# Attention and mixture of experts on one core: loads of q, k and v in pieces by head pair, and another order of TensorE's step

## The chip, the cores and the metric

The kernel runs on one core of a Trainium2 chip. The metric is the device time of one execution in microseconds, taken as the median of the runs.

## The reference

A windowed attention feeds a top-1 mixture of experts. Inputs q, k, v are float32 (8, 8, 576, 64); each token sees itself and the 63 before it.

```python
scores = q @ k.T / sqrt(64);  scores[not (0 <= i - j < 64)] = -1e9
attn = softmax(scores);       x = (attn @ v) as (4608, 512)
logits = (x/|x|) @ (emb/|emb|).T / tau          # 8 experts
e = argmax(logits);           gate = softmax(logits)[e]
out[token] = gate * (relu(x @ w1[e]) @ w2[e])   # w1[e] 512x1024, w2[e] 1024x512
```

## The kernel before

The work has two parts, one after the other. The first goes over the 4608 tokens in 36 tiles of 128 (two blocks of 64 queries each). It is written out by hand as steps: step `s` of `stages(s)` issues, for five tiles at once, the scores of tile `s`, the transposes of its exponentials for tile `s-1`, the values of tile `s-2`, the transposes of x for tile `s-3` and the logits of tile `s-4`. The order in which the calls stand is the order in each engine's queue, and each engine takes its queue strictly in turn. Every stage has one buffer in PSUM only (`score`, `pair`, `back`, `xback`), so a stage of the next step waits until the last step's has been read. Beside that, groups of four tiles get their expert (`choose`), their rank among its tokens (`ranks`, `ranks_out`), and are scattered to DRAM by GpSimd (`place`). The second part, from about 190 us on, runs the experts' two layers over slots of tokens, with weights loaded by SyncE, split into two halves by ScalarE and VectorE, and dense matmuls on TensorE.

What a step gives each engine, with line numbers of the profile of before:

- TensorE: scores (L188), values (L238, L243), logits (L297), transposes of x (L280), transposes of the exponentials (L220), and for some steps ranks (L334, L335).
- ScalarE: `own_scores` copies half of the scores out (L197), `xT_evac` evacuates x transposed (L284), `squares` (L273), `exponentials` (L211).
- VectorE: `all_scores` puts the other half in by a `copy_predicated` (L200), `maxima` (L204), `x_out` divides and writes x (L263 to L265), `attn_halves` masks the transposed exponentials into `aM` (L225), and the small operations on logits and ranks (`logits_out` L306, `choose`, `ranks_out`).
- GpSimd: `less_max` subtracts the maxima (L208), and `place`.

The loads of the first part stand on SyncE's queue. `load_qk(b)` brings q and k of one batch (nine blocks, four and a half steps) in two transfers, `load_v(b)` v in one; there are three buffers for q and k and two for v, and a transfer waits until TensorE has read what stood there. SyncE does nothing else, so nothing but these waits, and one for the landing of the eighth transfer before, holds it in a step.

```python
        for b in range(2, B):
            if s == (NB * (b - QB) + NB - 1) // 2 + 1:
                load_qk(b)
            if s == (NB * (b - VB) + NB - 1) // 2 + 3:
                load_v(b)
```

Here NB is 9, QB 3 and VB 2. One quarter of the experts' first weights (`w1raw`) is loaded in each of steps 7, 16, 25 and 30.

Ahead of the steps, q and k come in two parts (blocks 0 to 3, then the rest), with the constants `cs`, v, the experts' rows `er` (16 KB), `tb` and `ct`, and the last columns of the constants, which VectorE casts into `upper`. `expert_norms()` squares the experts' rows on ScalarE (L406), `expert_emb()` divides them on VectorE, `expert_emb_T()` transposes them on TensorE (L418) through `back`. `warm(n)` issues n small matmuls that nobody reads.

Of the kernel before, what the change touches and what calls it, by code (L numbers as in the profile page):

```python
# [22 lines left out]
B, H, S, D = 8, 8, 576, 64  # L23
N, DM, DF, E = 4608, 512, 1024, 8
WIN = 64
NB = S // WIN
# [56 lines left out]
def attention_moe(ctx, tc, q, k, v, emb, tau, w1, w2, kc, kt, out):  # L83
    nc = tc.nc
# [13 lines left out]
    def weave(*chains):  # L98

        chains = list(chains)  # L100
        while chains:
            chains = [c for c in chains if next(c, chains) is not chains]
# [21 lines left out]
    back, misc = (psa.tile([P, 512], F32, name=nm) for nm in ("back", "misc"))  # L124
# [30 lines left out]
    QB = 3  # L155
    qT, kT = ([aq.tile([P, 4, S], F32, name=f"{nm}{i}") for i in range(QB)] for nm in ("qT", "kT"))
    VB = 2
    vb = [av.tile([P, 4, NB, D + 1], F32, name=f"v{i}") for i in range(VB)]

    def load_qk(b, lo=0, hi=NB, engines=(nc.sync, nc.sync)):  # L160

        for engine, t, src in zip(engines, (qT, kT), (q, k)):
            engine.dma_start(t[b % QB][:, :, lo * WIN:hi * WIN], src[b, :, :, lo * WIN:hi * WIN].rearrange("u p s -> p u s"))

    def load_v(b, lo=0, hi=NB):
        nc.sync.dma_start(vb[b % VB][:, :, lo:hi], v[b, :, :, lo:hi].rearrange("u p a d -> p u a d"))

    def vblock(g):
        return vb[g // NB % VB][:, :, g % NB]
# [25 lines left out]
    def own_scores(T):  # L195
        sm[T] = ap.tile([P, 4, 2, WIN], F32, name="sm", bufs=3)
        nc.scalar.copy(sm[T], sv[:, :, :, 1])  # L197
# [4 lines left out]
    def maxima(T):  # L202
        st[T] = ap.tile([P, 8], F32, name="st", bufs=2)
        nc.vector.reduce_max(out=st[T], in_=sm[T].rearrange("p u h c -> p (u h) c"), axis=AX.X)  # L204

    def less_max(T):
        t = sm[T].rearrange("p u h c -> p (u h) c")
        nc.gpsimd.tensor_tensor(out=t, in0=t, in1=st.pop(T).unsqueeze(2).to_broadcast([P, 8, WIN]), op=ALU.subtract)  # L208
# [13 lines left out]
    def attn_halves(T):  # L222

        aM[T] = ap.tile([P, 2, 4, P], F32, name="aM", bufs=2)
        nc.vector.tensor_tensor(out=aM[T], in0=pT.pop(T).unsqueeze(1).to_broadcast([P, 2, 4, P]),  # L225
                                in1=halves.unsqueeze(2).to_broadcast([P, 2, 4, P]), op=ALU.mult)
# [3 lines left out]
    def values(T):  # L230

        px[T] = pair
        m = aM.pop(T)
        o, p = m[:, 0], m[:, 1]
        for u in range(4):
            for hp, z in sides:
                g, pr, pz = 2 * T + z, slice(64 * hp, 64 * hp + 64), slice(64 * z, 64 * z + 64)
                nc.tensor.matmul(pair[pz, hp, u * (D + 1):(u + 1) * (D + 1)], lhsT=o[pr, u, pz],  # L238
                                 rhs=vblock(g)[pr, u], start=True, stop=g % NB == 0)
            for hp, z in sides:  # L240
                g, pr, pz = 2 * T + z, slice(64 * hp, 64 * hp + 64), slice(64 * z, 64 * z + 64)
                if g % NB:
                    nc.tensor.matmul(pair[pz, hp, u * (D + 1):(u + 1) * (D + 1)], lhsT=p[pr, u, pz],  # L243
                                     rhs=vblock(g - 1)[pr, u], start=False, stop=True)
# [37 lines left out]
    def xT_evac(T):  # L282
        xT[T] = ap.tile([P, 4, P], F32, name="xT", bufs=2)
        nc.scalar.copy(xT[T], pxT.pop(T))  # L284
# [15 lines left out]
    def in_rows(G):  # L300

        return x_rows(*GROUPS[G])[:, :, C_LOG:C_LOG + E]

    def logits_out(G):
        a, b = GROUPS[G]
        nc.vector.tensor_copy(in_rows(G), plv[:, G % 2, :b - a])  # L306
# [51 lines left out]
    def rank_rows(G):  # L358
        a, b = GROUPS[G]
        n = b - a  # L360
        rk = ap.tile([P, n, E], F32, name="rk")
        at = [cs[:, K_E:K_E + E], *late][sum(a >= cut for cut in CUTS)]
        nc.vector.tensor_tensor(out=rk, in0=rank.pop(G), in1=at.unsqueeze(1).to_broadcast([P, n, E]), op=ALU.add)
        yield
        nc.vector.tensor_tensor(out=rk, in0=rk, in1=ohs.pop(G), op=ALU.mult)
        yield
        pos = ap.tile([P, n], F32, name="pos")
        nc.vector.reduce_sum(out=pos, in_=rk, axis=AX.X)
        yield
        rks[G] = ap.tile([P, n], I32, name="pi")  # L370
        nc.vector.tensor_copy(rks[G], pos)
        yield

    def ranks_out(G):
        weave(rank_rows(G))
# [14 lines left out]
    def root_guess(ss, t1):  # L390
        nc.gpsimd.tensor_tensor(out=t1, in0=ss, in1=half[:ss.shape[0]], op=ALU.pow)

    def root_refine(ss, t0, t1, o):

        nc.vector.tensor_scalar(out=t0, in0=t1, scalar1=1e-30, scalar2=None, op0=ALU.max)
        nc.vector.reciprocal(t1, t0)
        nc.vector.scalar_tensor_tensor(out=t1, in0=ss, scalar=t1, in1=t0, op0=ALU.mult, op1=ALU.add)
        nc.vector.tensor_scalar(out=o, in0=t1, scalar1=0.5, scalar2=1e-6, op0=ALU.mult, op1=ALU.add)
# [6 lines left out]
    def expert_norms():  # L405
        nc.scalar.activation(esq, er, AF.Square, accum_out=es[:, 0:1])  # L406
        root_guess(es[:, 0:1], es[:, 2:3])

    def expert_emb():
        root_refine(es[:, 0:1], es[:, 1:2], es[:, 2:3], es[:, 3:4])  # L410
        nc.vector.tensor_tensor(out=es[:, 0:1], in0=es[:, 3:4], in1=tb, op=ALU.mult)
        nc.vector.reciprocal(es[:, 1:2], es[:, 0:1])
        nc.vector.tensor_scalar(out=er2, in0=er, scalar1=es[:, 1:2], scalar2=None, op0=ALU.mult)
# [17 lines left out]
    def warm(n, to=back):  # L431

        for _ in range(n):
            nc.tensor.matmul(to[:, :P], lhsT=ones, rhs=ones, start=True, stop=True)

    def stages(s):

        def there(d):
            return 0 <= s - d < NT

        def ending(d):
            return [G for G, (a, b) in enumerate(GROUPS) if b + d == s]

        scores(s)
        if s < 3:
            warm(20, misc)
        own_scores(s)
        if there(2):
            tokens(s - 2)
            values(s - 2)  # L450
        if there(4):
            logits(s - 4)
        if there(3):
            x_transposes(s - 3)
            xT_evac(s - 3)
        all_scores(s)
        maxima(s)
        less_max(s)
        if there(3):
            squares(s - 3)  # L460
        for G in ending(3):
            logits_out(G)
        if there(2):
            x_out(s - 2)
        if s < 3:
            warm(20, misc)
        if there(1):
            attn_transposes(s - 1)
            attn_halves(s - 1)
        for G in ending(4):  # L470
            ranks(G)
            ranks_out(G)
        for G, (a, b) in enumerate(GROUPS):
            for T in range(a, b):
                if s == (T + 8 if b - a == 4 else b + 4):
                    place(T)
        for G in ending(3):
            choose(G)
            count(G)
        if s in wsplit:  # L480
            split_hi(wsplit[s], w1raw, w1h)
        exponentials(s)
        if s in wsplit:
            split_lo(wsplit[s], w1raw, w1h, w1l, nc.vector)
        if 1 <= s < 7:
            blanks(s - 1)

        for b in range(2, B):
            if s == (NB * (b - QB) + NB - 1) // 2 + 1:
                load_qk(b)  # L490
            if s == (NB * (b - VB) + NB - 1) // 2 + 3:
                load_v(b)
        for f in wsteps.get(s, ()):
            f()

# [422 lines left out]

    load_qk(0, 0, 4, (nc.sync, nc.scalar))
    nc.sync.dma_start(cs, kc[:, :K_U])  # L920
    load_v(0, 0, 4)
    load_qk(0, 4, NB, (nc.sync, nc.scalar))
    nc.sync.dma_start(er, emb)
    nc.sync.dma_start(tb, tau.to_broadcast([E, 1]))
    nc.sync.dma_start(ct, kt)
    nc.sync.dma_start(xbuf[2][:, :P], kc[:, K_U:])
    load_v(0, 4, NB)
    load_qk(1)
    load_v(1)
    nc.vector.memset(ones, 1.0)  # L930
    nc.vector.memset(low, -BIG / 64)
    nc.vector.memset(half, 0.5)
# [3 lines left out]
    nc.gpsimd.memset(xall[:, :, C_SS + 1:], 0.0)  # L936
    nc.gpsimd.memset(xmore[:, :, C_SS + 1:], 0.0)
    warm(60)
    expert_norms()

    buffers("xb", 2, [P, DM], F32, const)
    for name, shape, dtype in (("xh", [P, 4, 2 * P], F32R), ("xl", [P, 4, 2 * P], F32R)):
# [2 lines left out]
    for t in range(NT - 1):  # L945
        stages(t)
        if t == 0:
            nc.vector.tensor_copy(upper, xbuf[2][:, :P])
            expert_emb()
        if t == 1:  # L950
            expert_emb_T()
        if t == CUTS[0] + 4:
            sum_counts(CUTS[0])
            begin_late(0, counts("early"))
        if t == 30:
            load_x(0)
            load_x(1)
        if t in (32, 33):
            x_parts(t - 32)
# [4 lines left out]
    T, G = NT - 1, len(GROUPS) - 1  # L964
# [202 lines left out]
```

## Time and profile before

| | |
|---|---|
| time, median of 3 runs | 650.78 us (649.51 to 652.6) |
| profiled execution, own time / span | 653.34 / 651.6 us |
| busy: TensorE, VectorE, ScalarE, GpSimd | 93%, 68%, 51%, 31% of the span |
| mean granted TensorE clock | 0.978 |
| SyncE's queue (q1) | 120.08 MB, 56.8% of 16 engines |
| fetches of instructions (q8) | 58, 0.95 MB, 0.6% |
| one load: q, k, v of a batch | 1152 KB, 1152 KB, 1170 KB |
| one load: a quarter of w1 | 512 KB |

The profile is of one execution. A row of a timeline has the start, the time taken, the engine, the line, the operation, out<-in, and in brackets how long the engine had stood idle and what ended that. "issue" means that it waited for nothing that the profile shows. In a table of waits stand the microseconds in total, their number and the longest. In a table by stretches each engine has its busy time and the number of its instructions, and at the end stand the granted clock, the share of the DMA engines' time, and GB/s. The span is a little shorter than the execution's own time, which has what lies around it.

### The profile page before, as it was taken

The page shows a single profiled execution, that of the slowest core. Times are in us where ns is not written, and L with a number is a line of the kernel's source. Part 1 is how long each engine was busy: PE and PEld are TensorE (multiplying, and loading weights), DVE is VectorE, ACT ScalarE, POOL GpSimd, SP SyncE. Part 2 cuts the span into 40 slices and gives each one's busy share as a digit, 9 for nine tenths or more (in the row PEclk, how much of TensorE's full clock was granted, in tenths as well). Part 3 has the DMA queues.
Part 4 walks back from the last instruction along what each step waited for, and adds up shares of the span by engine and source line. Part 5 has one row for each costly group of instructions (what it writes and reads, how often), then busy time and mean ns, then how long its engine had stood idle before and what let it go on. Part 6 is the DMA issues. An engine that isn't in the chain of part 4 may idle for free. (4 is left out here: it accounts for less than half of the span.)

```text
span 651.6 us, 18205 instructions
## 1 busy us (share of the span) xinstructions
PE 605.4 (93%) x7178; PEld 541.9 (83%) x7178; DVE 443.3 (68%) x884; ACT 334.8 (51%) x513; POOL 202.0 (31%) x242
## 2 busy tenths in 40 slices
PE   6887888788789989999999999999999999999996
PEld 5776777677679978998998998998889988998984
DVE  1676895889968965767646887557665877567623
ACT  1343453445445244747544766547565576547533
POOL 1224544545464422322222331222122231222111
PEclk9998997989979999999999999999999999999999
DMA  9865476554442459987688688684798867694351
GB/s 286 323 226 212 162 274 218 210 210 159 148 152 80 162 129 301 304 283 229 212 255 291 220 268 288 211 293 157 244 301 267 288 194 271 201 305 175 116 163 36
DMA packets 83901, 143.77 MB, mean 221 GB/s; under 512 B 14421, under 2 KB 37717, under 8 KB 83808
## 3 DMA queue, kind: packets, MB, share of 16 engines
q1 hardware_dynamic: 76176, 120.08, 56.8%
q0 software_dynamic: 6000, 19.18, 7.5%
q10 hardware_dynamic: 1632, 3.28, 1.4%
q8 instruction: 58, 0.95, 0.6%
q14 instruction: 35, 0.29, 0.1%
HBM read 123.23 MB, written 20.05 MB: 220 GB/s over the span
## 5 line engine op out<-in xcount | busy, mean ns | idle before, releaser
L774 PE MATMUL ph<-xl,w1h 128*128 128x256 f32 x576 | 162.8, 283 | 2.0 <-POOL xl L676 2.0
L774 PE MATMUL ph<-xh,w1h 128*128 128x256 f32 x576 | 163.4, 284 | 0.0
L774 PE MATMUL ph<-xh,w1l 128*128 128x256 f32 x576 | 162.6, 282 | 0.0
L834 PE MATMUL po<-w2h,hl 128*128 128x512 f32 x312 | 122.9, 394 | 0.0
L834 PE MATMUL po<-w2h,hh 128*128 128x512 f32 x312 | 122.5, 393 | 0.0
L834 PE MATMUL po<-w2l,hh 128*128 128x512 f32 x312 | 122.3, 392 | 0.0
L844 POOL DMA_INDIRECT out<-o,rest x39 | 49.7, 1273 | 221.1 <-ACT o L843 215.7
L788 DVE SCALAR_TENSOR_TENSOR hl<-ph,hh 128x512 fp32r<-128x512 f32 x78 | 53.3, 689 | 93.5 <-ACT hh L784 93.3
L152 DVE TENSOR_TENSOR w2l<-w2raw,w2h 128x1024 fp32r<-128x1024 f32 x80 | 94.8, 1219 | 26.4 <-ACT w2h L149 26.2
L774 PEld LDWEIGHTS ph<-xl,w1h 128*128 128x128 f32 x576 | 109.9, 191 | 3.3 <-POOL xl L676 2.6
L774 PEld LDWEIGHTS ph<-xh,w1h 128*128 128x128 f32 x576 | 109.9, 191 | 1.2 <-issue 0.3
L774 PEld LDWEIGHTS ph<-xh,w1l 128*128 128x128 f32 x576 | 109.8, 191 | 0.0
L149 ACT CAST w2h<-w2raw 128x1024 fp32r<-128x1024 f32 x80 | 81.9, 1050 | 41.6 <-PE po L834 34.4
L152 DVE TENSOR_TENSOR w1l<-w1raw,w1h 128x1024 fp32r<-128x1024 f32 x80 | 95.5, 1248 | 11.2 <-ACT w1h L149 10.9
L676 POOL TENSOR_TENSOR xl<-xt,xh 128x512 fp32r<-128x512 f32 x39 | 51.1, 1312 | 103.1 <-ACT xh L672 103.1
L149 ACT CAST w1h<-w1raw 128x1024 fp32r<-128x1024 f32 x80 | 78.3, 1047 | 1.8 <-DMA w1raw<-in_w 1.8
L784 ACT ACTIVATE hh<-ph 128x512 fp32r<-128x512 f32 x78 | 46.0, 595 | 54.2 <-PE ph L774 39.3
L834 PEld LDWEIGHTS po<-w2h,hl 128*128 128x128 f32 x312 | 58.6, 188 | 13.0
L834 PEld LDWEIGHTS po<-w2l,hh 128*128 128x128 f32 x312 | 58.6, 188 | 12.7
L834 PEld LDWEIGHTS po<-w2h,hh 128*128 128x128 f32 x312 | 58.6, 188 | 12.2
L238 PE MATMUL pair<-v,aM 64*64 64x65 f32 x1152 | 40.2, 231 | 25.7 <-DVE aM L225 19.6
L238 PEld LDWEIGHTS pair<-v,aM 64*64 64x64 f32 x1152 | 33.6, 139 | 33.3 <-DVE aM L225 26.1
(171 smaller groups left out, 835.2 us busy)
## 6 DMA issues: line engine op xcount, KB each, us to landing
w2raw<-in_w SPq DMA_DIRECT2D x80, 512.0 KB, 6.0
w1raw<-in_w SPq DMA_DIRECT2D x76, 512.0 KB, 5.0
xb<-xs SPq DMA_DIRECT2D x156, 64.0 KB, 5.5
v<-in_v SPq DMA_DIRECT2D x7, 1170.0 KB, 5.6
qT<-in_q SPq DMA_DIRECT2D x7, 1152.0 KB, 6.7
kT<-in_k SPq DMA_DIRECT2D x7, 1152.0 KB, 9.3
w1raw<-in_w ACTq DMA_DIRECT2D x4, 512.0 KB, 4.4
v<-in_v SPq DMA_DIRECT2D x1, 650.0 KB, 5.0
```

What stands on the lines that cost most here:

```text
L149: nc.scalar.copy(hi[c], raw[c])
L152: eng.tensor_tensor(out=lo[c], in0=raw[c], in1=hi[c].bitcast(F32), op=ALU.subtract)
L238: nc.tensor.matmul(pair[pz, hp, u * (D + 1):(u + 1) * (D + 1)], lhsT=o[pr, u, pz], rhs=vblock(g)[pr, u], start=True, stop=g % NB == 0)
L676: nc.gpsimd.tensor_tensor(out=xl, in0=t, in1=xh.bitcast(F32), op=ALU.subtract)
L774: nc.tensor.matmul(o, lhsT=ww[c][:, f * P:(f + 1) * P], rhs=xx[:, c, :n], start=(c == 0 and i == 0), stop=(c == 3 and i == 2))
L784: nc.scalar.activation(hh, ph[g, part], AF.Relu)
L788: nc.vector.scalar_tensor_tensor(out=hl, in0=ph.pop((g, part)), scalar=0.0, in1=hh.bitcast(F32), op0=ALU.max, op1=ALU.subtract)
L834: nc.tensor.matmul(po[a], lhsT=xx[:, f, at], rhs=ww[f // 2][:, f % 2], start=(f == 0 and i == 0), stop=(f == 7 and i == 2))
L844: d = nc.gpsimd.indirect_dma_start(out=out, out_offset=bass.IndirectOffsetOnAxis(ap=tok, axis=0), in_=o, in_offset=None, bounds_check=N - ...
```

## The change

Four things are changed, and no arithmetic. The four transfers of head pairs that make up a batch's q, k or v become transfers of their own (`load_u` issues q and k of one pair, `load_vu` v of one pair), and a table `loads` puts them into steps: the four pairs of q and k into four steps in a row, the four of v into two. The small loads (`er`, `tb`, `ct`) go ahead of v and of the second part of q. The experts' norms go from ahead of step 0 to behind it, `expert_emb` and `expert_emb_T` one step later each. And the calls in a step stand in another order.

```diff
+    def load_u(b, u):
+        for t, src in ((qT, q), (kT, k)):
+            nc.sync.dma_start(t[b % QB][:, u], src[b, u])
+    def load_vu(b, u):
+        nc.sync.dma_start(vb[b % VB][:, u], v[b, u])
+    loads = {}
+    for b in range(2, B):
+        s0 = max(1, (NB * (b - QB) + NB - 1) // 2 + 1)
+        for u in range(4):
+            loads.setdefault(s0 + u, []).append(lambda b=b, u=u: load_u(b, u))
+        s0 = (NB * (b - VB) + NB - 1) // 2 + 3
+        for u in range(4):
+            loads.setdefault(s0 + u // 2, []).append(lambda b=b, u=u: load_vu(b, u))
...
             tokens(s - 2)
-            values(s - 2)
         if there(4):
             logits(s - 4)
         if there(3):
             x_transposes(s - 3)
-            xT_evac(s - 3)
+        if there(2):
+            values(s - 2)
+        for G in ending(3):
+            logits_out(G)
         all_scores(s)
         maxima(s)
+        if s < 3:
+            warm(20, misc)
+        if there(3):
+            xT_evac(s - 3)
         less_max(s)
...
         if there(1):
             attn_transposes(s - 1)
-            attn_halves(s - 1)
         for G in ending(4):
             ranks(G)
             ranks_out(G)
+        if there(1):
+            attn_halves(s - 1)
...
+        for f in loads.get(s, ()):
+            f()
...
     nc.sync.dma_start(cs, kc[:, :K_U])
-    load_v(0, 0, 4)
-    load_qk(0, 4, NB, (nc.sync, nc.scalar))
     nc.sync.dma_start(er, emb)
     nc.sync.dma_start(tb, tau.to_broadcast([E, 1]))
     nc.sync.dma_start(ct, kt)
+    load_v(0, 0, 4)
+    load_qk(0, 4, NB, (nc.sync, nc.scalar))
     nc.sync.dma_start(xbuf[2][:, :P], kc[:, K_U:])
     load_v(0, 4, NB)
-    load_qk(1)
-    load_v(1)
+    for u in range(4):
+        load_u(1, u)
+    for u in range(4):
+        load_vu(1, u)
...
     warm(60)
-    expert_norms()
...
         if t == 0:
             nc.vector.tensor_copy(upper, xbuf[2][:, :P])
+            expert_norms()
+        if t == 1:
             expert_emb()
-        if t == 1:
+        if t == 2:
             expert_emb_T()
```

The line numbers of the changed kernel are 17 to 19 higher. ScalarE's queue at the start, before: the square of the experts (into `xr`, where their rows lie) is ahead of the first copy of scores.

```order
L406 ACTIVATE xr,es<-xr 8x512
L197 COPY sm<-score 128x512
L211 ACTIVATE sm<-sm 128x512
L197 COPY sm<-score 128x512
L211 ACTIVATE sm<-sm 128x512
```

And now:

```order
L214 COPY sm<-score 128x512
L228 ACTIVATE sm<-sm 128x512
L423 ACTIVATE xr,es<-xr 8x512
L214 COPY sm<-score 128x512
L228 ACTIVATE sm<-sm 128x512
```

The square has moved behind the first tile's copy and exponential.

SyncE's queue from the q and k of batch 5 to those of batch 6, before (128 partitions, four head pairs, 576 tokens in one transfer):

```order
L163 DMA qT_118<-in_q 128x4x576
L163 DMA kT_121<-in_k 128x4x576
L166 DMA v_122<-in_v 128x4x585
L424 DMA w1raw_101<-in_w 128x1024
L163 DMA qT_116<-in_q 128x4x576
```

And now:

```order
L171 DMA qT_118<-in_q 128x576
L171 DMA kT_121<-in_k 128x576
L171 DMA qT_118<-in_q 128x576
L171 DMA kT_121<-in_k 128x576
L174 DMA v_122<-in_v 128x585 x2
L171 DMA qT_118<-in_q 128x576
L171 DMA kT_121<-in_k 128x576
L441 DMA w1raw_101<-in_w 128x1024
L174 DMA v_122<-in_v 128x585 x2
L171 DMA qT_118<-in_q 128x576
L171 DMA kT_121<-in_k 128x576
L171 DMA qT_116<-in_q 128x576
```

The last two pairs of q and k have moved behind pieces of the next v on the queue; every transfer is a quarter as long.

TensorE's queue in one step, from its scores to its transposes of exponentials, before (L238 and L243 are the values, `misc` holds the logits, `xback` x, `back` the exponentials):

```order
L188 MATMUL score<-kT_120,qT_117 64x128 x16
L238 MATMUL pair<-v_122,aM 64x65 x4
L243 MATMUL pair<-v_122,aM 64x65 x4
...
L297 MATMUL misc<-embT,xT 64x8 x8
L280 MATMUL xback<-cs,xr 128x128 x4
L220 MATMUL back<-cs,sm 128x128 x4
```

And now:

```order
L205 MATMUL score<-kT_120,qT_117 64x128 x16
L314 MATMUL misc<-embT,xT 64x8 x8
L297 MATMUL xback<-cs,xr 128x128 x4
L255 MATMUL pair<-v_122,aM 64x65 x4
L260 MATMUL pair<-v_122,aM 64x65 x4
...
L237 MATMUL back<-cs,sm 128x128 x4
```

The values have moved behind logits and x; scores and exponentials stand where they stood.

More of the change, by code (lines that the diff above doesn't have):

```diff
@@ L460, in stages @@
             squares(s - 3)
-        for G in ending(3):
-            logits_out(G)
         if there(2):
             x_out(s - 2)
-        if s < 3:
-            warm(20, misc)
         if there(1):
             attn_transposes(s - 1)
-            attn_halves(s - 1)
         for G in ending(4):
@@ L486, in stages @@
             blanks(s - 1)
[L488 to L492, printed above, removed]
+        for f in loads.get(s, ()):
+            f()
         for f in wsteps.get(s, ()):
```

## The prediction

> **What bounds the kernel now.** I read the page first, then the sums of waits, then VectorE's instructions step by step, and last the transfers around TensorE's waits. The page, the granted clock (40 slices of 16.3 us):
>
> ```profile
> PEclk9998997989979999999999999999999999999999
> ```
>
> After slice 12 the clock is full and TensorE (93% of the span) is the bound; the change leaves that part alone, so whatever the first 190 us gain or lose comes out at the end one for one. The dips are all in the attention steps. The sums of waits there:
>
> ```profile
> ACT xT L284 <- PE xback L280: 68.8, 31, 6.1
> DVE sm L200 <- ACT sm L197: 25.0, 19, 12.2
> PE pair L238 <- DVE aM L225: 19.6, 27, 1.9
> PE pair L238 <- issue: 6.1, 4, 2.2
> ```
>
> TensorE waits for VectorE in most steps, VectorE only now and then for ScalarE. So VectorE sets the steps' pace, and its own busy time is the floor. Rows of `copy_predicated` (L200, once a step) for steps 4, 13, 17 and 32, and VectorE's busy time (the pair of numbers after PEld) between the first and the last:
>
> ```profile
> 33.19 0.74 DVE L200 COPY_PREDICATED sm<-cs,score 128x512 f32<-128x512 uint32 x1 [0.22 <-ACT sm L197]
> 78.94 0.72 DVE L200 COPY_PREDICATED sm<-cs,score 128x512 f32<-128x512 uint32 x1
> 97.15 0.72 DVE L200 COPY_PREDICATED sm<-cs,score 128x512 f32<-128x512 uint32 x1
> 173.84 0.73 DVE L200 COPY_PREDICATED sm<-cs,score 128x512 f32<-128x512 uint32 x1
> 33.19:173.84 140.65, 116.64 (x3372) 102.75 (x3369) 114.32 (x243) 66.84 (x144) 64.35 (x104) 0.94 0.58 202
> ```
>
> Steps 13 to 17 took 18.21 us, 4.55 each, with no stall in them. 28 steps at 4.55 would be 127.4; they took 140.65. So 13.2 us of steps 4 to 32 are stalls. Where they are: the loads that the DMA queue issues, and TensorE's waits for nothing that the profile shows ("issue"):
>
> ```profile
> 34.89 0.39 SPq L163 DMA_DIRECT2D qT<-in_q  x1
> 44.03 0.39 SPq L166 DMA_DIRECT2D v<-in_v  x1
> 44.47 1.61 SPq L424 DMA_DIRECT2D w1raw<-in_w  x1
> 50.76 0.38 SPq L163 DMA_DIRECT2D qT<-in_q  x1
> 66.35 0.37 SPq L166 DMA_DIRECT2D v<-in_v  x1
> 95.85 0.37 SPq L163 DMA_DIRECT2D qT<-in_q  x1
> 123.04 0.37 SPq L163 DMA_DIRECT2D qT<-in_q  x1
> ...
> 43.15 0.28 PE L238 MATMUL pair<-v,aM 64*64 64x65 f32 x2 [1.23 <-issue]
> 52.80 0.29 PE L238 MATMUL pair<-v,aM 64*64 64x65 f32 x5 [0.60 <-issue]
> 59.28 0.37 PE L238 MATMUL pair<-v,aM 64*64 64x65 f32 x2 [2.08 <-issue]
> 103.56 0.38 PE L238 MATMUL pair<-v,aM 64*64 64x65 f32 x4 [2.17 <-issue]
> 130.39 0.29 PE L297 MATMUL misc<-embT,xT 128*64 128x8 f32 x5 [1.41 <-issue]
> ```
>
> Each wait but one stands 7 to 9 us behind a q load (a k load follows each at once: 2 x 1152 KB, 2.36 MB together); the 0.60 stands behind v with w1raw (1.7 MB). The v load alone (1.2 MB, at 66.35) is followed by none. What TensorE lacks are instructions. The transfers in 53.4 to 56.8 us (first two rows), and in 52 to 57 us (last):
>
> ```profile
> DMA packets 617, 1.38 MB, mean 407 GB/s; under 512 B 16, under 2 KB 16, under 8 KB 617
> q1 hardware_dynamic: 617, 1.38, 103.3%
> ...
> q8 instruction: 1, 0.02, 1.4%
> ```
>
> For 3.4 us nothing but q and k moved, 38 packets on each of 16 engines; only then came the one fetch of instructions (q8), too late for 57.2 us, where TensorE ran dry. The clock pays again (last three numbers: granted clock, DMA share, GB/s):
>
> ```profile
> 57.00:66.00 9.00, 6.92 (x138) 6.31 (x133) 4.01 (x7) 2.31 (x5) 3.56 (x5) 0.62 0.34 125
> 130.00:136.00 6.00, 5.61 (x118) 5.16 (x117) 3.96 (x11) 2.31 (x5) 2.47 (x6) 0.72 0.54 210
> ```
>
> The five waits sum to 7.5 us; the other 5.7 of the 13.2 are half clock and the refilling of the chain.
>
> **Part 1, the loads.** Twelve pieces of 0.29 MB for three transfers of 1.2 MB per batch. Bytes stay. SyncE isn't paced by the steps: it issues q and k of batch b as soon as the scores of b-3 free the buffer, at 0.37 to 0.5 us an issue. So the first two head pairs (four pieces, 1.18 MB over 1.8 us) still leave in one burst, of the size of a v load, which costs nothing now. The next v piece waits for TensorE's values and holds the other two pairs behind it on SyncE; nobody misses them, since they have eight steps until use (batch 4: freed in step 8, read in step 18). Then eight pieces, 2.38 MB, leave over some 3.4 us. In that time 407 GB/s drain about 1.0 MB (I allow 0.9 us until they flow), so the backlog peaks near 1.35 MB, between v alone (no wait) and v with w1raw (0.60). I take 0.4 us of loss for each of six such bursts, 2.4 in all: nearest to v's rows. Ends: 0, and 2.6 each (13.2 over five), if peak size means nothing. Term: -13.2 + 2.4 = -10.8.
>
> [...]
>
> **Part 2, the start.** Rows of TensorE, ScalarE and VectorE (`copy_predicated` of steps 0, 1 and 3), the issue of the constants' last columns and their landing (6.7 us later), and the mean times (ns, behind the busy us) of `attn_halves`, maxima and `x_out`:
>
> ```profile
> 6.31 1.10 PE L188 MATMUL score<-kT,qT 64*64 64x64 f32 x32
> 12.43 0.63 ACT L406 ACTIVATE xr<-xr 8x512 f32<-8x512 f32 x1 [9.09 <-DMA xr<-in_emb]
> 13.65 0.72 DVE L200 COPY_PREDICATED sm<-cs,score 128x512 f32<-128x512 uint32 x1 [12.22 <-ACT sm L197]
> 17.39 0.73 DVE L200 COPY_PREDICATED sm<-cs,score 128x512 f32<-128x512 uint32 x1
> 29.28 0.74 DVE L200 COPY_PREDICATED sm<-cs,score 128x512 f32<-128x512 uint32 x1 [1.36 <-ACT sm L197]
> 6.69 0.44 SPq L926 DMA_DIRECT2D xr<-in_kc  x1
> ...
> L225 DVE TENSOR_TENSOR aM<-back,cs 128x1024 f32<-128x1024 f32 x35 | 42.6, 1216 | 6.5 <-PE back L220 6.2 <-PE misc L335 0.2
> L204 DVE TENSOR_REDUCE st<-sm 128x8 f32<-128x512 f32 x36 | 24.7, 686 | 3.6
> L265 DVE TENSOR_TENSOR xr<-pair,sums 128x512 f32<-128x512 f32 x26 | 18.0, 691 | 1.1 <-DVE sums L264 0.2
> ...
> xr<-in_kc SPq DMA_DIRECT2D x1, 64.0 KB, 6.7
> ```
>
> The first scores are ready at 7.4, but ScalarE's square of the experts (L406) stands ahead of their copy and waits for its DMA until 12.43. Moved behind step 0, it frees copy and `copy_predicated` at about 8.0, 5.6 us earlier. What is late next: VectorE's cast of `upper`, in order ahead of step 1, needs the constants' last columns, which land at 13.4 as now (the same bytes stand ahead of them). The three small loads that now go ahead of v and of q's second part cost SyncE some 1.5 us of issues (0.5 each), but not a packet: the engines have work queued all through (share 1.00 in the row below). GpSimd's root of the experts moves behind its subtraction of step 0, where it idles. So step 1's `copy_predicated` comes at 13.6 instead of 17.39. Step 2's stands behind 0.73 + 0.69 + 1.22 of step 1 and the experts' chain (17.39 - 13.65 less 0.72 and 0.69 leaves 2.3 for `upper` and that chain; I take 2.1 for the chain), with gaps at 18.5. Then `expert_emb_T` on TensorE, now behind step 2's transposes, waits until `attn_halves` has read `back`: VectorE gets there at 22.5 (18.5, plus copy 0.73, maxima 0.69, `x_out` 0.69 and its two small operations, halves 1.22, and gaps), and transposes, scores (1.1) and ScalarE's copy follow: step 3's at some 24.8 against 29.28, 4.5 earlier. Against that, the queues are full:
>
> ```profile
> 5.00:31.00 26.00, 19.55 (x430) 17.45 (x430) 11.51 (x24) 5.61 (x11) 4.63 (x9) 0.93 1.00 346
> ```
>
> TensorE, now ahead, asks for its instructions while every engine is taken (share 1.00), where before it did so later. I take 1.5 off, one wait of the rows above. Term -3.0; ends -5.6 (the whole of the copy's advance) and 0.
>
> **Part 3, the step's order.** Values now come behind logits and x. Before, ScalarE's evacuation of x (L284) waits for TensorE, and square and exponential queue behind it:
>
> ```profile
> 53.80 1.04 POOL L208 TENSOR_TENSOR sm<-sm,st 128x512 f32<-128x512 f32 x1 [0.36 <-DVE sums L263]
> 55.56 0.62 ACT L211 ACTIVATE sm<-sm 128x512 f32<-128x512 f32 x1
> ```
>
> The exponential could have started at 54.84 and did at 55.56. With x transposed while TensorE used to wait for `aM`, it starts when GpSimd is done. That shortens the chain to the next copy by up to 0.7 us, but VectorE's busy time is 114.32 / 28 = 4.08 a step, about 4.3 with the gaps between instructions, against 4.55 now: at most 0.25 x 28 = 7 us. I take a third, since in most steps VectorE already runs without a wait: -2.5. Values end some 1.2 us later; VectorE needs them after `copy_predicated` and maxima, 1.5 us behind `aM`, so they stay hidden; if logits and x did not fit into TensorE's wait, each step would lose what doesn't fit. The filler matmuls (`warm`, steps 0 to 2 alone) keep their count: 0. `logits_out` ahead of `copy_predicated`, `ranks_out` ahead of `attn_halves`: same VectorE work, producers done earlier, 0. Steps 33 to 35 and the expert part: 0, within 1.5 either way for where the clock dips there.
>
> **Sum.** -10.8 - 3.0 - 2.5 = -16.3. The profiled execution took 653.3 us (span 651.6), 2.6 above the median of 650.8, which I take for scatter between runs: 637.0 for itself, 634.5 for the median.
>
> **Rivals.**
> A. All stalls go and the start keeps its lead: -13.2 - 4.5 - 4 = -21.7, 629. For it: v's bursts cost nothing now. Against: the second burst is larger than v's.
> B. The fetch's wait doesn't hang on how much is queued, so splitting changes nothing there, or the pieces rush out as one queue all the same: -3.0 - 2.5, 645. If an engine turned to the other queue after a packet or a few, each fetch would wait about as long in both kernels. Against: 38 packets an engine went by before the fetch. [...]
> C. Slower: the second burst of each batch stalls the fetch in full as q and k do now, and the first one too. Eleven bursts at 2.6 are 28.6 against 13.2, net of the gains +9.9: 660. It decides from (13.2 + 5.5) / 2.6, more than seven full stalls, on. For it: 2.38 MB in a row; against: they come over 3.4 us, not one.
> D. B, and the start's lead lost to full queues: 648 to 651, no change.
>
> **Numbers.** The forecast 0.60, A 0.15, B 0.14, C 0.05, D 0.06. Half a per cent (3.3 us) is about what a measurement of this kernel can tell from none. Faster 0.89, same 0.06, slower 0.05. The range goes from within A (626) to B (646) and leaves out C, D and the edge of A.
>
> **What would show it.** Step 0's copy on ScalarE at about 7.5 and VectorE waiting for the constants' DMA at `upper`; TensorE's waits on "issue" in the attention steps 3 us or less instead of 7.5, the clock at 1.00 from 35 to 170 us; `copy_predicated` of step 32 near 158; the wait of `xT` for TensorE far below 68.8. Wrong it is if "issue" waits of 2 us stand behind the v bursts (C), or behind the first pieces (B), or if VectorE begins to wait for `pair` in every step.

## The result

| | before | after |
|---|---|---|
| time, median | 651.3 us (649.51 to 652.6, 4 runs) | 634.88 us (632.41 to 636.99, 4 runs) |
| in a second comparison | 651.79 us (11 runs) | 639.23 us (633.79 to 642.02, 6 runs) |
| profiled execution, own time / span | 653.34 / 651.6 us | 635.14 / 633.4 us |

The ratio is 0.9748 [0.9705, 0.9791], and 0.9783 [0.974, 0.9827] in the second comparison: 14 to 16 us faster by the ratios. The forecast was 634.5; the first median stands 0.4 from it, the second 4.7. The profile after, granted clock in 40 slices, then the sums of waits that answer to those of before:

```profile
PEclk9997999999899999999999999999999999999999
ACT xT L301 <- PE xback L297: 13.8, 23, 2.5
DVE sm L217 <- ACT sm L214: 13.0, 10, 7.5
```

ScalarE's wait for x fell from 68.8 to 13.8 us, and the dips are fewer, not gone. The rows of `copy_predicated` (now L217) of steps 0, 1, 3, 4, 13, 17 and 32, with the cast of `upper` ahead of step 1:

```profile
8.92 0.73 DVE L217 COPY_PREDICATED sm<-cs,score 128x512 f32<-128x512 uint32 x1 [7.49 <-ACT sm L214]
13.91 0.23 DVE L965 CAST upper<-xr 128x128 bf16<-128x128 f32 x1 [3.54 <-DMA xr<-in_kc]
14.05 0.72 DVE L217 COPY_PREDICATED sm<-cs,score 128x512 f32<-128x512 uint32 x1
23.94 0.74 DVE L217 COPY_PREDICATED sm<-cs,score 128x512 f32<-128x512 uint32 x1 [1.55 <-ACT sm L214]
27.83 0.75 DVE L217 COPY_PREDICATED sm<-cs,score 128x512 f32<-128x512 uint32 x1 [0.20 <-ACT sm L214]
68.90 0.73 DVE L217 COPY_PREDICATED sm<-cs,score 128x512 f32<-128x512 uint32 x1
86.50 0.73 DVE L217 COPY_PREDICATED sm<-cs,score 128x512 f32<-128x512 uint32 x1
158.36 0.72 DVE L217 COPY_PREDICATED sm<-cs,score 128x512 f32<-128x512 uint32 x1
```

Step 4 comes at 27.83 against 33.19 (-5.4). Steps 4 to 32 take 130.53 us against 140.65 (-10.1). From step 32 to the end it is 475.0 against 477.8 (-2.7). Together -18.2 between these two executions. Steps 13 to 17 take 17.60, 4.40 each against 4.55. So 28 steps without a stall would be 123.2, and 7.3 us of stalls are left of 13.2.

TensorE's waits on "issue" between 25 and 155 us did not go: 3.0, 2.5 and 1.2 against 6.1, 1.4 and 0.6.

```profile
PE pair L260 <- issue: 3.0, 2, 1.9
PE misc L314 <- issue: 2.5, 2, 1.7
PE score L205 <- issue: 1.2, 2, 0.9
PE pair L255 <- DVE aM L242: 1.6, 4, 0.5
```

Those for `aM` did: 1.6 us, against 12.8 of before between the same times.

The longest wait on issue, and SyncE's queue ahead of it:

```profile
36.00 0.81 SPq L174 DMA_DIRECT2D v<-in_v  x2
38.51 0.43 SPq L441 DMA_DIRECT2D w1raw<-in_w  x1
40.84 0.43 SPq L171 DMA_DIRECT2D kT<-in_k  x1
41.62 0.33 SPq L171 DMA_DIRECT2D qT<-in_q  x1
43.86 0.33 SPq L171 DMA_DIRECT2D kT<-in_k  x1
...
45.89 0.28 PE L260 MATMUL pair<-v,aM 64*64 64x65 f32 x3 [1.86 <-issue]
```

Five rows stand for the thirteen transfers issued from 36.00 on. The second burst (four pieces of batch 2's v, four of batch 3's q and k, w1raw) ends at 41.3, and batch 4's first four pieces, whose buffer has just come free, follow at 41.62: 4 MB in 8 us. The transfers from 40.0 to 43.4 us, and the fetch among those from 43.4 to 45.0:

```profile
q1 hardware_dynamic: 497, 1.25, 100.3%
...
q8 instruction: 1, 0.02, 3.8%
```

For 3.4 us nothing but loads moved, as before the change. The prediction had the two bursts apart.

### The profile page after: what moved, and what is told of

Same layout as the page of the kernel before. It is cut to its first block, busy times and chain, and to the rows that moved or that the text cites. A ratio compares the mean times of both kernels' runs of the same rounds, so it can differ in the third digit from the quotient of the medians.

```text
span 633.4 us, 18301 instructions
## 1 busy us (share of the span) xinstructions
PE 605.2 (96%) x7178; PEld 536.0 (85%) x7178; DVE 441.1 (70%) x884; ACT 336.4 (53%) x513; POOL 202.5 (32%) x242
## 5 line engine op out<-in xcount | busy, mean ns | idle before, releaser
L225 POOL TENSOR_TENSOR sm<-sm,st 128x512 f32<-128x512 f32 x36 | 37.5, 1041 | 67.3 <-DVE sums L280 35.0
L688 ACT CAST xh<-xt 128x512 fp32r<-128x512 f32 x39 | 24.2, 620 | 59.7 <-DVE xt L677 58.9
```

The lines of the kernel that those rows point to most:

```text
L688: nc.scalar.copy(xh, t)
```

## The experiments

The times of before beside them were 652.15 us (the first four), 651.79 (the next four), 653.67 (aligned and shifted) and 653.66 (the last). The sums of waits on issue are TensorE's, between 25 and 155 us.

**The parts, each alone.** Before with the new start:

```diff
     nc.sync.dma_start(cs, kc[:, :K_U])
+    nc.sync.dma_start(er, emb)
+    nc.sync.dma_start(tb, tau.to_broadcast([E, 1]))
+    nc.sync.dma_start(ct, kt)
     load_v(0, 0, 4)
...
-    expert_norms()
...
             nc.vector.tensor_copy(upper, xbuf[2][:, :P])
+            expert_norms()
+        if t == 1:
             expert_emb()
...
```

> Before with the changes at the start alone: small loads ahead of v, the experts' norms behind step 0, expert_emb and expert_emb_T a step later each. My theory: the changed kernel's copy_predicated of step 4 came at 27.83 us against 33.19, so the start is worth 5.4 us, 646 against 651.3; the prediction had 3.0. Rival (the start's lead is given back in the steps behind it, since TensorE asks for its instructions while the DMA engines are full): 649 to 651. Either way the five waits on issue stay about as they were, 7.5 us in sum.

646.0 us, ratio 0.9917 [0.9884, 0.995]: -5.4. Step 4's `copy_predicated` came at 27.54. The lead isn't given back.

Before with the loads in pieces:

```diff
-                load_qk(b)
...
-                load_v(b)
+        for f in loads.get(s, ()):
+            f()
...
```

> Before with the loads of q, k and v in pieces by head pair, spread over steps, and nothing else. My theory (fetches of instructions queue behind what the loads have put into the DMA engines; smaller bursts, shorter waits): 6 us of stalls go, 645; the prediction's term was 10.8, 640.5. Rival (the pieces run together, since the second half of a batch's pieces and the first of the next leave back to back, and the waits of the changed kernel, 6.75 us against 7.5, show that splitting gains nothing): 650 to 652, with four to six waits of 1 to 2 us on issue.

648.7 us, ratio 0.9925 [0.9883, 0.9967]: -4.9, between theory and rival. Steps 4 to 32 took 135.78 us, 8.4 above 28 x 4.55. The waits on issue sum to 5.1 us, against 8.1 in before.

Before with the new order:

```diff
-            values(s - 2)
...
             logits(s - 4)
...
             x_transposes(s - 3)
...
+            values(s - 2)
...
-            attn_halves(s - 1)
...
             ranks(G)
...
+            attn_halves(s - 1)
```

> Before with the new order of the calls in a step and nothing else. My theory: 0.15 us a step over 28 steps (4.55 to 4.40 in the steps without a stall) and some 2 us at the end of the steps: 645 to 647, with copy_predicated of steps 13 and 17 about 17.6 us apart. Rival (the order is what gains the middle, since TensorE then has work that doesn't hang on aM and stalls cost the chain less): 10 us, 641, with the loads and their waits on issue as before.

651.08 us, ratio 1.0005 [0.9973, 1.0036]: nothing, and both expectations missed. Where nothing stalls, a step is shorter: steps 27 to 30 took 13.69 us against 14.31. Steps 13 to 17 took 18.39, not 17.6, with two waits on issue (1.4 and 0.7) in them. The waits sum to 6.7 us, no more than the 8.1 of before; what grew is the time at half clock. The clock and the stretch of steps 4 to 32:

```profile
PEclk8888997979999999999999999999999999999999
33.65:173.31 139.66, 122.88 (x3358) 103.08 (x3355) 114.22 (x244) 70.05 (x147) 65.15 (x104) 0.91 0.58 202
```

139.66 us less 28 x 4.40 leaves 16.5 of stalls, against 13.2 in before. The granted clock is 0.91 there against 0.94.

The new start and the new order, with the large loads of before:

```diff
-        for f in loads.get(s, ()):
-            f()
+        for b in range(2, B):
+            if s == (NB * (b - QB) + NB - 1) // 2 + 1:
+                load_qk(b)
+            if s == (NB * (b - VB) + NB - 1) // 2 + 3:
+                load_v(b)
...
```

> The changed kernel with the large loads of before (one transfer for q, one for k, one for v of a batch, at their old steps). My theory: the stalls of the large loads come back, 6 us, so 641 against 634.9. Rival (splitting gains nothing, the start and the order carry the whole): 634 to 636, the same as the changed kernel, with waits on issue of 7 us in sum.

642.86 us, ratio 0.9883 [0.9849, 0.9916]: -7.6. Theory 1 holds: by the ratios the changed kernel is 6.5 to 8.8 us faster than this one, so the pieces carry that much on top of start and order. Its waits on issue, which sum to 12.6 us; the three largest groups:

```profile
PE pair L243 <- issue: 4.4, 3, 2.0
PE xback L280 <- issue: 3.6, 2, 3.0
PE score L188 <- issue: 2.8, 2, 1.6
```

The changed kernel has 6.7. Steps 4 to 32 took 136.96 us here and 130.53 there, at the same granted clock of 0.96: 6.4 us, about what the waits differ by. Beside the kernel with the new start alone (646.0), this one tells the order's worth with large loads: 2 to 3 us, not clear of noise.

The new start and the pieces, with the old order of a step (the diff of the order alone, the other way round):

> The changed kernel with the old order of the calls in a step (new start, loads in pieces). What is open: start -5.4, loads -4.9 and order +0.3, each alone, sum to -10.0, the whole change gave -16.4. Theory 1 (the parts don't add because the order leaves TensorE no slack: it shortens a step by 0.15 us where nothing is late, and loses that again where fetches are late; with smaller bursts there is less to lose): 641, so that the order is worth 6 here though nothing alone; steps 13 to 17 at 4.55 us each. Rival (start and loads add to more than their sum, since a start 5 us earlier also moves the fetches against the bursts; the order is worth nothing): 635 to 637, with steps of 4.55.

643.82 us, ratio 0.987 [0.9825, 0.9915], against 639.23 of the changed kernel beside it: the order is worth 4.6 here by medians, 5.7 by the ratios. This speaks for theory 1, but the intervals just overlap. The waits on issue sum to 5.8 us; with large loads, the new start and the old order they were 7.6.

**Where the fetches stand.** The changed kernel itself, nothing edited, once more:

> The changed kernel itself, beside the others on the same chip: 635 (ratio 0.975). Its waits on issue need not stand at the same steps as in the first profile if small shifts in time decide them; their sum should be about 6.75 us again.

639.23 us, as above, 4 over what was expected. The execution that was profiled took 642.02, 6.9 above the first, with almost the same waits (7.4 us on issue against 6.7) but more of the slow clock. TensorE's busy time is the number behind the window's length, the granted clock the third from the end. Three stretches of the first execution, then four of this one:

```profile
44.19:47.60 3.41, 1.71 (x59) 1.60 (x63) 2.21 (x6) 1.04 (x3) 1.97 (x6) 0.99 1.04 394
47.60:51.01 3.41, 3.41 (x53) 2.73 (x48) 3.20 (x8) 0.59 (x1) 1.38 (x2) 0.50 0.47 178
51.01:54.43 3.42, 3.42 (x80) 2.97 (x84) 1.52 (x5) 1.84 (x4) 2.23 (x3) 0.51 0.22 80
```

```profile
47.78:51.19 3.41, 2.12 (x55) 1.55 (x51) 2.94 (x6) 1.79 (x4) 1.50 (x3) 1.00 0.79 303
51.19:54.60 3.41, 2.82 (x50) 2.36 (x53) 1.36 (x4) 0.63 (x1) 2.10 (x3) 0.50 0.25 85
54.60:58.02 3.42, 3.42 (x49) 2.74 (x44) 1.98 (x3) 0.59 (x1) 0.00 (x0) 0.50 0.01 4
58.02:61.43 3.41, 3.41 (x77) 2.95 (x80) 1.53 (x5) 1.89 (x4) 2.23 (x3) 0.50 0.46 100
```

In these records the clock changed only at the edges of windows of 3.41 us, all on one grid within an execution: in the first one at 47.56, 54.39, 91.93 and 95.35 us (2, 11 and 1 windows apart), in before at 59.09, 65.92, 103.47 and 110.29 (2, 11 and 2). The grid lies elsewhere in each. Here a window in which TensorE was busy for 1.71 or 2.12 us of 3.41 was followed by windows at half speed, though no single wait reached 2 us. The six executions differ in the same way: the two with a mean clock of 0.994 took 633.8 and 634.5 us, the four with 0.980 to 0.983 took 638.6 to 642.0.

The changed kernel with each fetch moved half a step against the loads:

```diff
-    warm(60)
+    for _ in range(124):
+        nc.tensor.matmul(back[:, :64], lhsT=ones, rhs=ones[:, :64], start=True, stop=True)
```

> The changed kernel with 124 filler matmuls of 64 columns in place of 60 of 128 at the start (the same time, 6.2 us), so that every fetch of TensorE's instructions, one for each 256 of them, comes 128 instructions, about half a step, earlier against the loads. Theory 1 (where a fetch falls in a burst decides how late it is): other waits on issue at other steps, and a time 2 to 5 us away from the changed kernel's, 630 to 640, either way. Rival (the waits are set by the loads alone): the same time within 1 us, 634 to 636.

641.84 us, ratio 0.9805 [0.9752, 0.9858]. The waits moved, now 1.8 us at 49.5 and 2.2 us at 96.9, and sum to 6.4. By the ratios the time is 1.4 above the kernel beside it (0.9783), too little to tell from the scatter. It shows that the place moves, not what it costs.

The changed kernel, with SyncE held to the steps:

```diff
             tokens(s - 2)
+            if s in loads:
+                nc.gpsimd.memset(tick[:, s:s + 1], 0.0)
...
+        if s >= 2 and s in loads:
+            nc.sync.dma_start(ticks[s:s + 1], tick[:, s:s + 1])
         for f in loads.get(s, ()):
```

> The changed kernel, and SyncE made to keep to the steps: ahead of each step's loads from step 2 on stands a transfer of 4 bytes from a word that GpSimd sets in that step, so that SyncE can't issue a step's loads before it. Theory 1 (the second half of a batch's pieces and the first of the next leave together, 3 to 4 MB in a row, and the fetches of instructions wait behind them): waits on issue of 2 us or less in sum where the changed kernel had 6.75, and 3 to 5 us faster than it, 630 to 632 against 635. Rival (the fetches wait for any load, however short the queue): 634 to 636 and some 6 us of waits on issue. It could also be slower, if v then comes late: TensorE's values waiting for the DMA of v.

635.8 us, ratio 0.9753 [0.9715, 0.979]: not to be told from the changed kernel. The waits on issue still sum to 6.2 us (nine, the longest 1.5), so theory 1 missed here. Fetches still waited here, behind the short queue that one step's pieces make; one case is in the transfers from 50.1 to 52.2 us, loads and GpSimd's scatter (q0) with no fetch among them (it began at 52.2), and the wait that followed:

```profile
q1 hardware_dynamic: 269, 0.54, 76.1%
q0 software_dynamic: 36, 0.15, 18.1%
...
54.52 0.27 PE L255 MATMUL pair<-v,aM 64*64 64x65 f32 x2 [0.52 <-issue]
```

How little delay it takes can be estimated from the traces. In all profiles but that of the last kernel below, the waits on issue over 0.15 us between 20 and 190 us, 71 of them, end 1.2 to 1.6 us behind the landing of a fetch of 16 KB, and they stand at multiples of 128 matmuls (each with its weight load: 256 instructions) from each other, within five. (The profile after has 58 such fetches, 0.95 MB, for 7178 matmuls and 7178 weight loads.) The next fetch never began less than 1.0 us behind such a wait, and a fetch took 0.9 us at the least. So, as an estimate which takes the next block's fetch to be asked for when TensorE enters a block of 256 instructions, a fetch that nothing holds up is ready some 3.1 to 3.5 us after that (1.0, 0.9 and 1.2 to 1.6). A block lasts some 4.7 us where nothing stalls (28 steps of 4.38 us in the kernel below hold 3360 matmuls). That leaves 1.2 to 1.6 us: by this estimate a shorter queue still makes TensorE wait as soon as it holds the fetch up for longer.

If it holds, what matters is not only how much is queued but whether the fetch comes before it or behind it. The next kernel schedules the loads for that. `LOADS` gives for each block of 256 instructions the place of a step where TensorE enters it and the pieces to release there; `ungate` stands behind `xT_evac`, `less_max`, `squares` and `exponentials`:

```diff
+    LOADS = {
+        ('lm', 15): (14, [['v', 4, 0], ['v', 4, 1], ['v', 4, 2]]),
...
+    def ungate(spot, s):
+        if (spot, s) in LOADS:
+            i, pieces = LOADS[spot, s]
+            if spot == "lm":
+                nc.gpsimd.memset(tick[:, i:i + 1], 0.0)
+            else:
+                nc.scalar.copy(tick[:, i:i + 1], half[:1])
+            nc.sync.dma_start(ticks[i:i + 1], tick[:, i:i + 1])
+            for p in pieces:
+                load_one(*p)
```

> The changed kernel with a schedule of its loads by TensorE's fetches instead of by steps: q, k, v and w1raw of steps 3 to 30 in pieces (of 0.29 MB, w1raw 0.5), three or four to each block of 256 instructions of TensorE, released by a 4-byte transfer as in the paced kernel, whose word is set by GpSimd or ScalarE at that place of a step which stands within 0.9 us of the moment when TensorE enters a block and asks for the next one. The fetch so starts ahead of the pieces, and they have some 4 us to drain before the next. Theory 1 (a fetch waits for what the loads have queued ahead of it): waits on issue of 1.5 us or less in sum between 25 and 155 us, against 6.2 to 7.4 in the changed and the paced kernel, no half clock there, 28 steps at 4.4 us, and 628 to 632 us. Rival (the wait is the fetch's own latency, or the stalls only move to VectorE and GpSimd): 5 us or more of waits on issue, or 634 to 638 us.

629.68 us (627.59 to 632.07), ratio 0.9647 [0.961, 0.9683], as theory 1 had it, and below both intervals of the changed kernel. It is the fastest version here. Its waits on issue, its steps 4 to 32 with a clock of 1.00, and one release (w1raw and a piece of q, 0.8 MB) with what moved from 101.3 to 103.6 us, the fetch among it:

```profile
PE score L243 <- issue: 0.6, 1, 0.6
```

```profile
28.34:151.00 122.66, 113.18 (x3360) 94.94 (x3359) 113.44 (x243) 71.13 (x163) 65.29 (x113) 1.00 0.78 247
```

```profile
100.96 0.25 SPq L219 DMA_DIRECT2D ticks<-tick  x1
101.26 0.33 SPq L178 DMA_DIRECT2D w1raw<-in_w  x1
101.64 0.44 SPq L182 DMA_DIRECT2D qT<-in_q  x1
...
q8 instruction: 1, 0.02, 2.4%
```

28 steps took 4.38 us each, as the steps without a stall did in the changed kernel (4.40). The paced kernel, also without half clock there, took 128.84: 6.2 us more, with 5.6 us more of waits on issue.

The same pieces, released half a block later:

> The same schedule of pieces as in the aligned kernel, each release about 2.3 us later, half a block of TensorE's instructions, so that the next fetch comes while the pieces drain. Theory 1: the fetches wait again, 5 us or more on issue in sum between 25 and 155 us, 634 to 641 us, slower than the aligned kernel by 4 to 8. Rival (what helps is the even spread, three pieces at a time, and not where they stand against the fetches): the same as the aligned kernel within 2 us.

638.35 us, ratio 0.9782 [0.9746, 0.9817], 8.7 slower than the aligned kernel, with the same pieces in the same groups: the place of the releases alone (and with it which engine sets each word). The waits on issue are 3.5 us against 0.6, less than the 5 that were expected, and one for `kT` grew from 1.0 to 2.1. Steps 4 to 32 took 128.74, 6.1 more. A fetch asked for at about 103.5 us, by the estimate above: the transfers until 106.3, with no fetch among them, and TensorE behind it:

```profile
q1 hardware_dynamic: 257, 0.53, 57.6%
q0 software_dynamic: 80, 0.27, 23.8%
...
108.80 0.29 PE L293 MATMUL pair<-v,aM 64*64 64x65 f32 x5 [1.43 <-issue]
```

GpSimd's scatter (q0, 23.8%) is among them too. Of what else lies between the two, the records show one window at half clock in step 31, at 150.5 us, and two behind step 32, at 171 and 222; the aligned kernel has one behind step 32, at 156, and none from step 4 to there.

The aligned kernel with the old order in a step:

> The aligned kernel with the old order of the calls in a step; its releases are put anew to the moments at which TensorE, in that order, enters a block. What is open: the order alone gave nothing (ratio 1.0005), though a step without a stall took 4.40 us with it and 4.55 without. Theory 1 (the order's 0.15 us a step is real and is lost again only where fetches come late, because TensorE then has no other waits to hide them in): with next to no late fetches the whole 28 x 0.15 = 4.2 us shows, and some 2 us at the end of the steps, so this kernel takes 634 to 636 against 629.7 of the aligned one. Rival (the order is worth nothing at all, and the shorter steps are paid elsewhere): 629 to 631.

641.46 us, ratio 0.9822 [0.9787, 0.9857], 11.8 slower than the aligned one: the rival falls, but the size is twice theory 1's. The profile puts 5.7 us of waits here on issue too, but these are of another kind. All ten ahead of values, 5.5 us of them, end within 0.06 us behind VectorE's `aM`, and nine of them have no fetch that landed 1.2 to 1.6 us before. One of them, with `aM` done at 71.79:

```profile
70.57 1.22 DVE L280 TENSOR_TENSOR aM<-back,cs 128x1024 f32<-128x1024 f32 x1
71.84 0.35 PE L293 MATMUL pair<-v,aM 64*64 64x65 f32 x8 [0.81 <-issue]
```

So fetches are hardly ever late here, and TensorE waits for VectorE, as in before. Steps 4 to 32 and 13 to 17:

```profile
27.40:159.79 132.39, 111.23 (x3372) 97.19 (x3372) 114.43 (x244) 69.81 (x166) 63.61 (x107) 0.99 0.73 232
67.71:86.39 18.68, 15.35 (x482) 13.36 (x477) 16.90 (x37) 10.40 (x25) 9.64 (x16) 1.00 0.78 249
```

A step takes 4.67 here, not 4.55: in this order ScalarE's evacuation of x is late, and the words that ScalarE sets for SyncE (23 of 26, against 16 in the aligned kernel; some stand behind `own_scores` here) seem to lie on its chain. That is 28 x 0.12 = 3.4 us which the releases add, an estimate, since no run takes them off ScalarE. Between the two profiles lie 9.7 us in steps 4 to 32 (132.39 less 122.66) and 4.5 behind step 32. Of the 9.7, by the same estimate, 28 x (4.55 - 4.38) = 4.8 are the order's, 3.4 the releases', and 1.5 are left; one window at half clock (0.99 in the row, 1.00 in the aligned kernel's) can account for that. So the order is worth more here than beside late fetches, but the run doesn't part it cleanly from the releases.

## Why the prediction was right, and where its steps were off

The total held (-16.3 forecast, -16.4 and -12.6 measured by medians), its terms less so, and that it held is in part luck: the loads gave less than forecast, the start more, and the order nothing alone but some 5 us beside the pieces. Of its own signs two failed: the waits on issue are 6.7 us and not 3 or less, and the clock in steps 4 to 32 is 0.96 and not 1.00.

**Part 1, loads: -10.8 forecast.** Measured -4.9 alone, 6.5 to 8.8 on top of the other parts, and in the first profile 7.3 us of stalls left where 2.4 were forecast. The mechanism is shown by the aligned and the shifted kernel, which differ in nothing but where the releases stand: late fetches (0.6 and 3.5 us of waits on issue), and the clock behind them (1.00 and 0.99 in steps 4 to 32). What failed is the step "I take 0.4 us of loss for each of six such bursts". It took a batch's two bursts as apart, and at 41.62 the next batch's first pieces joined the second. And it took the fetch's wait to shrink with the queue to nothing, where 17 packets an engine (269 over 16), with some of GpSimd's, still meant 0.52 us of wait in the paced kernel. The trace of before already spoke against size alone: the q and k of batch 4, as large as the other bursts, cost 0.17 us, and of the four times that v went with w1raw (44.03, 88.96, 135.50, 154.87) only the first was followed by a wait.

```profile
77.63 0.37 SPq L163 DMA_DIRECT2D qT<-in_q  x1
...
86.18 0.87 PE L188 MATMUL score<-kT,qT 64*64 64x128 f32 x18 [0.17 <-issue]
```

Rival B (splitting changes nothing) fell all the same. Under the same start and order, the pieces have fewer waits each time: 5.1 against 8.1 us, 5.8 against 7.6, 6.7 (7.4 in the second profile) against 12.6. But splitting and spreading by steps doesn't take them away.

**Part 2, the start: -3.0 forecast, -5.4 measured,** near its end of -5.6. Step 0's `copy_predicated` at 8.92, the wait for the constants (13.91) and step 1 at 14.05 came nearly as worked out (8.0, 13.4, 13.6), and step 3's at 23.94 where 24.8 was. The step that failed is "I take 1.5 off": TensorE has no wait on issue there. That its other waits cover the late fetch is likely but not shown.

**Part 3, the order: -2.5 forecast.** It would save 4.2 us in steps without a stall (0.15 x 28), and it saves some 2 behind step 32, which I had put at 0: step 35 follows step 34 after 4.38 us, where it took 6.29 (4.39 with the new order alone, 6.27 with the new start alone).

```profile
171.40 0.73 DVE L217 COPY_PREDICATED sm<-cs,score 128x512 f32<-128x512 uint32 x1 [1.17 <-ACT sm L214]
175.78 0.74 DVE L217 COPY_PREDICATED sm<-cs,score 128x512 f32<-128x512 uint32 x1
```

But alone, with large loads, it gives that back to half clock (0.91 against 0.94 in steps 4 to 32) and shows nothing. The likeliest reason, argued and not shown: between 25 and 155 us TensorE had 12.8 us of waits for `aM` to hide a late fetch in, and now has 1.6. With the new start it shows up as waits: 12.6 us on issue with the new order against 7.6 with the old. The terms were added as if they were independent; the order's worth hangs on the loads. Step 32 near 158 and `xT`'s wait came as said.

**The clock.** The prediction read two dips (0.62 and 0.72) as the price of waits of 2.08 and 1.41 us, and the rows above agree: in the window of 3.41 us that holds the wait of 1.86 us, 1.71 us of work didn't keep the clock up, and it was 0.50 in the next.

Rival C did not come: no burst stalled in full more often than before. Rival A's 629 is near what the aligned kernel reached (629.68), by another way.

## What to carry to other kernels

Where an engine's long instruction stream stalls on "issue", look at which transfers stand ahead of its fetch. Cutting them up was worth 5 to 9 us here and left over half of the waits; releasing them about when the fetch starts took nearly all of the rest away (6.7 to 0.6 us, and the time from 634.9 to 639.2 down to 629.7). Measure a reordering together with the stalls around it, not alone: here it was worth nothing that can be told from noise in the kernel before, 2 to 3 us with the new start, some 5 with the pieces too, and more with the loads aligned, though there the releases have a part in it.

## What the runs showed that was not expected

The granted clock went window by window. Over the 13 profiles, up to 190 us, each execution was taken along its grid of 3.41 us. 46 windows at full clock were followed by one at half: in all of them TensorE was busy for 63% or less, in 31 for half or less. No window below 47% was followed by full clock. In between the busy share doesn't decide: of the windows busy for more than half and up to 63%, 15 were followed by half clock and 28 by full. One to three half windows followed, even where TensorE was busy all through the first (3.41 of 3.41 at 47.60); why one here and two there, the records don't show. The grid lies elsewhere in each execution, and nearly the same waits came with more or fewer half windows: the changed kernel's two profiles had 4 and 7 of them before 190 us, and 7 us between their spans. That the grid's place makes this difference is argued, not shown.
